# Thresholded attention with a hardswish MLP: an order in periods of two slots for the work between the score matmuls

## The chip, the cores and the metric

The kernel runs on one core of a Trainium2 chip. The metric is the device time of one launch. Before the change three runs took 568.69, 568.73 and 570.11 us; the median is 568.73 us. The profiled execution took 568.41 us, of which 566.6 us lie between its first and its last instruction, at a mean granted TensorE clock of 0.994.

## What is computed

Eight batches of eight heads, 576 rows, head size 64, then an MLP on the joined heads (512 to 2048 to 512):

```python
scores = q @ k.T / 8                              # per head, 576 x 576
thresh = max(scores, -1) - tau                    # tau = 0.02
scores = where(scores >= thresh, scores, -1e9)
attn = exp(scores - max(scores, -1)); attn /= sum(attn, -1) + 1e-9
x = (attn @ v), heads joined                      # 4608 x 512
h = x @ w_in                                      # 4608 x 2048
out = (h * clip(h + 3, 0, 6) / 6) @ w_out         # 4608 x 512
```

## The kernel before

The 64 heads form 32 pairs and 16 quads (a quad is four heads, two pairs of one batch). A quad has nine slots. Slots 0 to 3 are the four blocks of 128 rows of its first pair, slots 4 to 7 those of its second, and slot 8 holds the last 64 rows of all four heads. A slot is one tile of 128 rows by 2 x 576 columns: head `a=0` and head `a=1`. There are 144 slots, numbered n.

The order is written out by hand; no scheduler moves anything. Each engine works through its own queue in the order in which the loop `for n, sl in enumerate(queue)` issues instructions, and semaphores tie the queues. One turn of the loop handles several slots at once:

- ScalarE: the exponentials of slot n-1 (`sm_exp`, L311), a rectifier of the MLP if it falls to ScalarE (`mm1_relu`, L386), then the threshold of slot n (`sm_mask`, L306).
- VectorE: the row maxima of slot n+1 (`sm_max`, L299; they also copy the scores out of PSUM), the copies left in `waiting`, a rectifier if it falls to VectorE (L388), the gate (`mm1_gate`, L401), the reciprocal of slot n-1's row sums (`sm_recip`, L314), then the transposes of q and k for later quads (L238, L244, one VectorE instruction each), and the copies out of PSUM of the attention product (`av_main` L354, `av_rest` L364) and of the output (`osb`, L420).
- GpSimd: the bias of the threshold (L302) and the normalisation of slot n-1 (`sm_norm`, L319), whose result a transposing DMA on SyncE's queue brings into `pT` or `pR` for the attention product (L327).
- TensorE: one `mm1` item (L378, eight matmuls of 256 columns, or L373, four of 512), in even slots two parts of `mm2` (L412, eight matmuls of 512), the products `av_main` (slots 3 and 8, L343 and L346) and `av_rest` (slot 4), and the scores (L284).

From slot N1 = 22 on the scores are issued in odd slots only, those of slot n+3 first and then those of n+2: `for m in (n + 3, n + 2): scores(m)`. The copies in `waiting` run in odd slots only (at the end of an odd slot, or after the maxima of the next slot when they arose in an even one). Two sets of PSUM columns hold scores. Even slots use one set, odd slots another, and `scores(m)` can start when `sm_max(m-2)` has read its set:

```python
def score_col(n, a):
    return (704 if first(n) else 128) + (0 if a else 1536)
```

The last 256 columns of an odd slot's scores lie in banks 2 and 5. These two banks also serve, in turns (`bank()`), the products of `av` and the transposes by TensorE. `mm1` has one bank, HB = 6, so the next `mm1` waits for the gate of the last; `mm2` has bank 7.

The loads of q and k are prepared by `load_quad` and started one after another at the end of a slot (`start(loads, 1)`, SyncE's queue). For quads 0 to 3 TensorE transposes q and k (`by_pe`), for later quads VectorE does, 128 x 576 at a time; the last 64 rows of k (`transpose_rest`, L254) always go through TensorE, and ScalarE copies them out (L219, two copies).

Which slots have the rectifier on ScalarE, and when the transposes come, is written as sets of slots:

```python
r = mm1_relu(h, on_act=(slot in ((0, 2, 4, 8) if quad < 2 * NB else (0, 1, 3, 4) if quad % 2 else (0, 4, 5, 8))))
t0 = 3 if quad % 2 and quad > 1 else 4
t1 = -1 if quad % 2 == 0 and quad > 2 else 0 if quad else 1
```

`t0` is the slot of a quad in which q of the next quad's first pair is transposed, followed by its k and the rest; `t1` and `t1 + 1` are the slots of q and k of a quad's own second pair, with q one slot ahead at some quad borders. Since a quad has nine slots, these slots have both parities. After the loop a tail finishes the MLP of the last batches.

Of the kernel before, what the change touches and what calls it, by code (L numbers as in the profile page):

```python
# [20 lines left out]
def kernel(  # L21
# [17 lines left out]
    NQUAD = B * H // 4  # L39
    NSLOT = 9  # L40
    NB = 2
    N1 = 22
# [28 lines left out]
    qkT = {}  # L71
# [124 lines left out]
    def alloc_qk(quad):  # L196
        qkT[quad] = (qk_pool.tile([P, 2, S], F32, tag="qT", name="qT"),
                     qk_pool.tile([P, 2, S + 64], F32, tag="kT", name="kT"))

    def qT_of(pair):  # L200
        return qkT[pair // 2][0][:, pair % 2, :]

    def kT_of(pair):
        return qkT[pair // 2][1][:, pair % 2, :]
# [17 lines left out]
    def by_pe(pair):  # L222
        return pair // NPAIR < NB
# [8 lines left out]
    def transpose_q(pair):  # L232
        nq = nat[pair // 2][0]
        if by_pe(pair):
            pb = main_pe(nq[:, 0:1024].rearrange("p (t h d) -> p t h d", h=4, t=4), pair)
            return lambda: nc.vector.tensor_copy(out=qT_of(pair)[:, 0:512], in_=pb)
        n = pair % 2
        nc.vector.transpose(out=qT_of(pair), in_=nq[:, n * S:(n + 1) * S])  # L238

    def transpose_k(pair):  # L240
        if not by_pe(pair):
            n = pair % 2
            km = nat[pair // 2][1][:].rearrange("p t h d -> p (t h d)")
            nc.vector.transpose(out=kT_of(pair)[:, 64:576], in_=km[:, n * 512:(n + 1) * 512])  # L244
            return None
        pb = main_pe(nat[pair // 2][1], pair)
        return lambda: copy_out(kT_of(pair)[:, 64:576], pb)
# [43 lines left out]
    def sm_max(sl):  # L291
        sl.s = s_pool.tile([P, 2, S], F32, tag="s", name="s")
        sl.m = stat_pool.tile([P, 2], F32, tag="m", name="m")
        sl.bias = stat_pool.tile([P, 2], F32, tag="bias", name="bias")
        sl.rsum = stat_pool.tile([P, 2], F32, tag="rsum", name="rsum")
        sl.rinv = stat_pool.tile([P, 2], F32, tag="rinv", name="rinv")
        for i in range(2):
            c0 = score_col(sl.n, i)
            nc.vector.tensor_scalar(out=sl.s[:, i, :], in0=ps_flat[:, c0:c0 + S],  # L299
                                    scalar1=1.0, scalar2=None, op0=Alu.mult, op1=Alu.max,  # L300
                                    accum_out=sl.m[:, i:i + 1])
        nc.gpsimd.tensor_scalar(out=sl.bias[:], in0=sl.m[:], scalar1=-scale, scalar2=tau, op0=Alu.mult, op1=Alu.add)  # L302
# [10 lines left out]
    def sm_recip(sl):  # L313
        nc.vector.reciprocal(out=sl.rinv[:], in_=sl.rsum[:])  # L314
# [15 lines left out]
    def pe_transpose(sl):  # L330
        pb = ps_flat[:, HB * 512:HB * 512 + S].bitcast(BF16).rearrange("p (c t) -> p c t", t=P)
        pn = sl.pn[:].rearrange("p a b -> p (a b)")
        for c in range(9):
            nc.tensor.transpose(pb[:, c, :], pn[:, c * P:(c + 1) * P], identb[:])
        return lambda: nc.vector.tensor_copy(out=sl.dst, in_=pb)
# [47 lines left out]
    def mm1_relu(hps, on_act):  # L383
        r = r_pool.tile([P, 512], F32, tag="r", name="r")[:]
        if on_act:
            nc.scalar.activation(out=r, in_=hps, func=Act.Relu, bias=three[:])  # L386
        else:
            nc.vector.tensor_scalar(out=r, in0=hps, scalar1=3.0, scalar2=0.0, op0=Alu.add, op1=Alu.max)  # L388
        return r

    def mm1_gate(item, hps, r):
        b, ni, c0 = item
        if c0 is None:
            if ni % 8 == 0:
                odd[0] = go_pool.tile([P, 1024], BF16, name="go")
            out = odd[0][:, ni % 8 * P:ni % 8 * P + 512]
        else:
            c0 += (b % 2) * (S + 64)
            out = gbuf[:, ni:ni + 2, c0:c0 + 256]
            r, hps = (x.rearrange("p (n w) -> p n w", n=2) for x in (r, hps))  # L400
        nc.vector.scalar_tensor_tensor(out=out, in0=r, scalar=6.0, in1=hps, op0=Alu.min, op1=Alu.mult)  # L401
        if c0 is None and ni % 8 == 4:
            nc.sync.dma_start_transpose(out=gbuf[:, ni - 4:ni + 4, 512:512 + P], in_=odd[0][:])
# [45 lines left out]
    evict = transpose_k(0)  # L449
# [25 lines left out]
    sm_max(queue[0])  # L475
    scores(1)

    prev = None
    part = 0
    waiting = []  # L480
    for n, sl in enumerate(queue):
        quad, slot = sl.quad, sl.slot
        b, g = divmod(quad, 2)
        now = n
        if slot in (0, 4):
            pts[2 * quad + slot // 4] = pt_pool.tile([P, 9, 512], BF16, tag="pT", name="pT")
        if slot == 8:
            ptr[quad] = ptr_pool.tile([P, 9, P], BF16, tag="pR", name="pR")
        for ahead in {0: (1, 2), 9: (3,), 16: (4,)}.get(n, (quad + 2,) if quad > 2 and slot == 4 else ()):
            if ahead < NQUAD:  # L490
                load_quad(ahead)
        if slot == 0 and g == 1 and b + 1 < B:
            load_v(b + 1)
        if prev is not None:
            for i in range(2):
                sm_exp(prev, i)
        if n + 1 < len(queue):
            sm_max(queue[n + 1])
        for copy in waiting:
            copy()  # L500
        waiting = []

        if todo1:
            item, then = todo1.pop(0)
            h = mm1(item)
            r = mm1_relu(h, on_act=(slot in ((0, 2, 4, 8) if quad < 2 * NB else (0, 1, 3, 4) if quad % 2 else (0, 4, 5, 8))))
            mm1_gate(item, h, r)
            todo2.extend(then)
        copies = pe_transpose(queue[n - 2]) if n > 1 and queue[n - 2].on_chip else None
        if prev is not None:  # L510
            sm_recip(prev)
        if copies:
            copies()
        for _ in range(2 if n % 2 == 0 and todo2 else 0):
            bb, mt, part = todo2.pop(0)
            mm2_part(bb, mt, part)
        for i in range(2):
            sm_mask(sl, i)
        evict = []
        nxt = 2 * quad + 2  # L520
        t0 = 3 if quad % 2 and quad > 1 else 4
        t1 = -1 if quad % 2 == 0 and quad > 2 else 0 if quad else 1
        if slot == t1 or slot == 8 and quad % 2 and 1 < quad < NQUAD - 1:
            evict.append(transpose_q(2 * (quad + slot // 8) + 1))
        if slot == t1 + 1:
            evict.append(transpose_k(2 * quad + 1))
        if n == 3:
            evict.append(transpose_rest(0, of_k=False))
        if slot == 3 and quad > 0:
            waiting.append(av_main(2 * quad - 1))  # L530
        elif slot == 4 and quad > 0:
            waiting.append(av_rest(quad - 1))
            if quad % 2 == 0:
                todo1.extend(moe_of(quad // 2 - 1))
        if t0 <= slot < t0 + 3 and quad + 1 < NQUAD:
            if slot == t0:
                alloc_qk(quad + 1)
                evict.append(transpose_q(nxt))
            elif slot == t0 + 1:
                evict.append(transpose_k(nxt))  # L540
            else:
                evict.append(transpose_rest(quad + 1))
        if slot == 8:
            waiting.append(av_main(2 * quad))
        for out_of_psum in evict:
            if out_of_psum:
                out_of_psum()
        if part == 3:
            waiting.append(lambda tile=(bb, mt): late.extend(mm2_out(*tile, on_act=False)))
            part = 0  # L550
        if n < N1 or n % 2:
            for copy in waiting:
                copy()
            waiting = []
        if n == 0:
            warm_up(8)
        if n <= N1:
            scores(n + 2)
        elif n % 2:
            for m in (n + 3, n + 2):  # L560
                if m < len(queue):
                    scores(m)
        if n < 8:
            warm_up(6)
        if prev is not None:
            sm_norm(prev)
        flush()
        if n == 0:
            start(loads, 2)
        elif n not in (4, 12, 15, 18, 21) and not 23 < n < 34:  # L570
            start(loads, 1)
        if n < 4 or 15 < n < 20 or n > 33:
            start(vcasts, 1)
        else:
            start(casts, 2 if n in (5, 8, 11, 14) or 21 < n < 28 else 1)
        prev = sl
# [80 lines left out]
```

## Time and profile before

| what | value |
|---|---|
| median of three runs | 568.73 us |
| TensorE busy | 532.5 us |
| ScalarE busy | 450.4 us |
| VectorE busy | 444.0 us |
| GpSimd busy | 277.2 us |
| row maxima, L299 | 288 x 749 ns |
| threshold, L306; exponential, L311 | 288 x 763 ns; 288 x 670 ns |
| gate, L401 | 128 x 687 ns to `g`, 16 x 687 ns to `go` |
| rectifier on VectorE, L388; on ScalarE, L386 | 67 x 685 ns; 77 x 685 ns |
| reciprocal, L314 | 144 x 158 ns |
| transposes on VectorE, q L238; k L244 | 24 x 757 ns; 24 x 692 ns |
| normalisation, L319 | 288 x 745 ns |
| VectorE's maxima idle for scores (L284) | 40.4 us |
| ScalarE's rectifier idle for mm1 (L378) | 48.5 us |
| VectorE's gate idle for ScalarE's rectifier | 24.0 us |

Durations of neighbours on one engine overlap a little, so the pace, from start to start, is shorter than the duration: the two maxima of a slot start 0.68 us apart at 0.75 us each. Idle time of an engine costs something only if its next instruction lies on the path that sets the end. A matmul counts as busy while it waits in the array behind another one, so TensorE's share of busy time is not its share of peak.

### The profile page before, as it was taken

To read this page: it belongs to the slowest core of one execution; us is meant where nothing else is said; L and a number is where in the kernel's file an instruction comes from. 1 tells how busy PE (TensorE), PEld (TensorE's weight loads), DVE (VectorE), ACT (ScalarE), POOL (GpSimd) and SP (SyncE) were. 2 spreads that over 40 slices of the span, in tenths; PEclk is the share of its full clock that TensorE was granted. 3 is DMA by queue.
4 is the path that set the end of the run, shared out by engine and by line. 5 is a ranking of instruction groups with operands and counts; after the bars stand their busy time and mean duration, and the time that the engine had idled before them with its cause. 6 is when DMAs were issued, how large, how long until landed. Compare 5 with 4: busy or idle time off the path is not lost.

```text
span 566.6 us, 11592 instructions
## 1 busy us (share of the span) xinstructions
PE 532.5 (94%) x3865; PEld 321.2 (57%) x3865; DVE 444.0 (78%) x1099; ACT 450.4 (79%) x977; POOL 277.2 (49%) x502
## 2 busy tenths in 40 slices
PE   8999988999968999999999999999999999999997
PEld 6765555655535556556555556556555556664663
DVE  3788878888876988888888988888888898882541
ACT  3999969888988788878898888977897888991540
POOL 1788868556463445644455454644355444460000
PEclk9999999999988999999999999999999999999999
DMA  5999989779999768987899878987789875553212
GB/s 120 135 162 152 169 136 186 121 124 160 177 158 171 142 117 145 184 142 137 148 148 184 154 133 139 188 148 142 129 142 193 155 133 111 104 104 97 60 35 74
DMA packets 316587, 78.73 MB, mean 139 GB/s; under 512 B 299504, under 2 KB 312048, under 8 KB 316528
## 3 DMA queue, kind: packets, MB, share of 16 engines
q1 hardware_dynamic: 297920, 68.69, 68.6%
q0 software_dynamic: 17408, 8.92, 14.4%
q8 instruction: 30, 0.49, 0.4%
q10 hardware_dynamic: 1200, 0.39, 0.3%
q14 instruction: 29, 0.24, 0.1%
HBM read 36.70 MB, written 9.44 MB: 81 GB/s over the span
## 4 chain that ended last, share of the span: by engine, by line
PE 45%; DVE 23%; issue 7%; ACT 6%; DMA 4%; POOL 2%; SPq 2%; POOLq 0%; DVEq 0%
PE ps L284 17%; PE ps L378 12%; DVE s L299 10%; PE ps L412 9%; PE ps L343 3%; ACT r L386 3%; DVE r L388 3%; DVE g L401 3%; POOL pn L319 2%; DMA pT<-pn 2%; ACT s L306 2%; DVE qT L238 2%; ACT s L311 1%; DVE kT L244 1%; DVE rinv L314 1%
## 5 line engine op out<-in xcount | busy, mean ns | idle before, releaser
L319 POOL TENSOR_SCALAR pn<-s,rinv 128x576 bf16<-128x576 f32 x288 | 210.9, 745 | 153.9 <-DVE rinv L314 63.7
L299 DVE TENSOR_SCALAR_CACHE_REDUCE s<-ps 128x576 f32<-128x576 f32 x288 | 205.3, 749 | 47.7 <-PE ps L284 40.4
L306 ACT ACTIVATE s<-s,bias 128x576 f32<-128x576 f32 x288 | 205.9, 763 | 6.3 <-POOL bias L302 6.0
L284 PE MATMUL ps<-kT,qT 64*128 64x192 f32 (+7 forms) x1280 | 193.9, 422 | 8.5 <-DVE s L299 4.7
L311 ACT ACTIVATE s<-s 128x576 f32<-128x576 f32 x288 | 192.5, 670 | 0.3
L284 PEld LDWEIGHTS ps<-kT,qT 64*128 64x128 f32 (+1 forms) x1280 | 116.4, 176 | 75.1 <-DVE s L299 23.1
L378 PE MATMUL ps<-xT,w_in_sb 128*128 128x256 bf16 x1024 | 131.3, 274 | 6.7 <-DVE g L401 5.1
L412 PE MATMUL ps<-w_out_sb,g 128*128 128x512 bf16 x576 | 133.5, 379 | 0.0
L378 PEld LDWEIGHTS <-w_in_sb 128*128 128x128 bf16 x1024 | 94.6, 98 | 51.5 <-issue 36.5
L401 DVE SCALAR_TENSOR_TENSOR g<-r,ps 128x512 bf16<-128x512 f32 x128 | 87.9, 687 | 26.1 <-ACT r L386 24.0
L386 ACT ACTIVATE r<-ps,three 128x512 f32<-128x512 f32 x77 | 52.7, 685 | 59.1 <-PE ps L378 48.5
L412 PEld LDWEIGHTS <-g 128*128 128x128 bf16 x576 | 56.2, 98 | 57.8 <-issue 0.7
L302 POOL TENSOR_SCALAR bias<-m 128x2 f32<-128x2 f32 x144 | 27.1, 188 | 78.0 <-DVE s L299 59.0
L311 ACT ACTIVATION_READ_ACCUMULATOR s<-s 128x1 f32 x288 | 54.5, 189 | 0.0
L388 DVE TENSOR_SCALAR r<-ps 128x512 f32<-128x512 f32 x67 | 45.9, 685 | 0.6 <-PE ps L378 0.6
L420 DVE TENSOR_SCALAR osb<-ps 128x512 f32<-128x512 f32 x31 | 21.2, 684 | 24.4 <-PE ps L412 24.4
L343 PE MATMUL ps<-pT,vm 128*64 128x512 bf16 x256 | 34.6, 393 | 3.6 <-DMA pT<-pn 3.6
L343 PEld LDWEIGHTS <-vm 128*64 128x64 bf16 x512 | 18.1, 112 | 25.7 <-issue 16.0
L354 DVE CAST xT<-ps 128x512 bf16<-128x512 f32 x32 | 21.7, 679 | 4.5 <-PE ps L346 3.7
L299 DVE DVE_READ_ACCUMULATOR s<-ps 128x1 f32 x288 | 23.8, 83 | 0.0
L219 ACT COPY kT<-ps 64x128 f32<-64x128 f32 (+1 forms) x29 | 8.5, 293 | 18.3 <-PE ps L254 11.0
L314 DVE RECIPROCAL rinv<-rsum 128x2 f32<-128x2 f32 x144 | 22.7, 158 | 0.0
(56 smaller groups left out, 242.0 us busy)
## 6 DMA issues: line engine op xcount, KB each, us to landing
out_dram<-osb SPq DMA_DIRECT2D x31, 256.0 KB, 2.5
nq<-in_q_dram SPq DMA_DIRECT2D x96, 72.0 KB, 3.0
km<-in_k_dram SPq DMA_DIRECT2D x96, 64.0 KB, 2.8
vm<-in_v_dram POOLq DMA_DIRECT2D x16, 256.0 KB, 5.3
km<-in_k_dram SPq DMA_DIRECT2D x16, 128.0 KB, 4.3
w_in_sb<-in_moe_w_in_dram POOLq DMA_DIRECT2D x16, 128.0 KB, 4.5
w_out_sb<-in_moe_w_out_dram POOLq DMA_DIRECT2D x16, 128.0 KB, 4.3
pT<-pn SPq DMA_TRANSPOSE x117, 3.5
```

What stands on the lines that cost most here:

```text
L284: nc.tensor.matmul(ps_flat[rows, c0:c0 + w], qT_of(pair)[a * 64:(a + 1) * 64, q0:q0 + rows.stop - rows.start], kT_of(pair)[a * 64:(a + 1) ...
L299: nc.vector.tensor_scalar(out=sl.s[:, i, :], in0=ps_flat[:, c0:c0 + S], scalar1=1.0, scalar2=None, op0=Alu.mult, op1=Alu.max, accum_out=sl ...
L306: nc.scalar.activation(out=s, in_=s, func=Act.Prelu, bias=sl.bias[:, i:i + 1], scale=scale, alpha=REJECT)
L311: nc.scalar.activation(out=s, in_=s, func=Act.Exp, accum_out=sl.rsum[:, i:i + 1])
L314: nc.vector.reciprocal(out=sl.rinv[:], in_=sl.rsum[:])
L319: nc.gpsimd.tensor_scalar(out=pn[:, i, :], in0=sl.s[:, i, :], scalar1=sl.rinv[:, i:i + 1], scalar2=1.0, op0=Alu.mult, op1=Alu.mult)
L343: nc.tensor.matmul(pb[a * 64:(a + 1) * 64, :], vm[:, 2 * hp + a, c * D:(c + 1) * D], pT[:, 5 * a + c, cols], start=(c == 0), stop=False)
L378: nc.tensor.matmul(ps[:, hb, n * 256:(n + 1) * 256], w_in_sb[:, ki, (ni + n) * P:(ni + n + 1) * P], xT[b][:, ki, c0:c0 + 256], start=(ki = ...
L386: nc.scalar.activation(out=r, in_=hps, func=Act.Relu, bias=three[:])
L388: nc.vector.tensor_scalar(out=r, in0=hps, scalar1=3.0, scalar2=0.0, op0=Alu.add, op1=Alu.max)
L401: nc.vector.scalar_tensor_tensor(out=out, in0=r, scalar=6.0, in1=hps, op0=Alu.min, op1=Alu.mult)
L412: nc.tensor.matmul(o_ps[0], gbuf[:, ni, mt * P:(mt + 1) * P], w_out_sb[:, ni, :], start=(ni == 0), stop=(ni == NI - 1))
```

## The change

The order is given a period of two slots from slot 22 on. Even slots hold only the maxima, the rectifier and the gate on VectorE. Odd slots hold all transposes of q and k, the copies, the reciprocals of two slots and, on GpSimd, the norms of two slots; their rectifier is made by ScalarE, and their gate comes after the transposes. So that all transposes fall on odd slots, a table `turns` gives the slot of each: for quad 3 and later, every second slot from `first_odd` on, in the order q, k, rest, q, k. This starts up to four slots earlier than before, so `load_quad` of quad 6 and later is called at slot 0 in place of slot 4. The aim is to take out of even slots what the next odd slot's maxima would wait for.

```diff
+    turns = {1: [("q", 1)], 2: [("k", 1)], 3: [("rest", 0)]}
...
+    for quad in range(1, NQUAD):
+        n0 = quad * NSLOT
+        first_odd = n0 - 9 + quad % 2
+        for i, (job, of) in enumerate((("q", 2 * quad), ("k", 2 * quad), ("rest", quad),
+                                       ("q", 2 * quad + 1), ("k", 2 * quad + 1))):
+            turn_at(n0 + (-5, -4, -3, 0, 1)[i] if quad < 3 else first_odd + 2 * i, job, of)
+
     prev = None
+    ready = []
...
-        for ahead in {0: (1, 2), 9: (3,), 16: (4,)}.get(n, (quad + 2,) if quad > 2 and slot == 4 else ()):
+        for ahead in {0: (1, 2), 9: (3,), 16: (4,)}.get(n, (quad + 2,) if quad > 2 and slot == (4 if quad == 3 else 0) else ()):
...
             sm_max(queue[n + 1])
+        even = n >= N1 and n % 2 == 0
+        for old in ready:
+            sm_recip(old)
         for copy in waiting:
             copy()
         waiting = []
 
+        gate = None
         if todo1:
             item, then = todo1.pop(0)
             h = mm1(item)
-            r = mm1_relu(h, on_act=(slot in ((0, 2, 4, 8) if quad < 2 * NB else (0, 1, 3, 4) if quad % 2 else (0, 4, 5, 8))))
-            mm1_gate(item, h, r)
+            r = mm1_relu(h, on_act=not even)
+            gate = lambda: mm1_gate(item, h, r)
             todo2.extend(then)
+        if gate and even:
+            gate()
         copies = pe_transpose(queue[n - 2]) if n > 1 and queue[n - 2].on_chip else None
-        if prev is not None:
+        if prev is not None and n < N1:
             sm_recip(prev)
...
-        nxt = 2 * quad + 2
-        t0 = 3 if quad % 2 and quad > 1 else 4
-        t1 = -1 if quad % 2 == 0 and quad > 2 else 0 if quad else 1
-        if slot == t1 or slot == 8 and quad % 2 and 1 < quad < NQUAD - 1:
-            evict.append(transpose_q(2 * (quad + slot // 8) + 1))
-        if slot == t1 + 1:
-            evict.append(transpose_k(2 * quad + 1))
-        if n == 3:
-            evict.append(transpose_rest(0, of_k=False))
+        for job, of in turns.get(n, ()):
+            if job == "k":
+                evict.append(transpose_k(of))
+            elif job == "q":
+                if of // 2 not in qkT:
+                    alloc_qk(of // 2)
+                evict.append(transpose_q(of))
+            else:
+                evict.append(transpose_rest(of, of_k=of > 0))
+        if n >= N1 and not even:
+            sm_recip(prev)
+            if gate:
+                gate()
...
-        if t0 <= slot < t0 + 3 and quad + 1 < NQUAD:
-            if slot == t0:
-                alloc_qk(quad + 1)
-                evict.append(transpose_q(nxt))
-            elif slot == t0 + 1:
-                evict.append(transpose_k(nxt))
-            else:
-                evict.append(transpose_rest(quad + 1))
...
         if prev is not None:
-            sm_norm(prev)
+            ready.append(prev)
+        if not even:
+            for old in ready:
+                sm_norm(old)
+            ready = []
```

## The prediction

> **What bounds the kernel now.** I read the busy times first, then the windows, then one pair of slots in order of time, then the waits.
>
> ```profile
> PE 532.5 (94%) x3865; PEld 321.2 (57%) x3865; DVE 444.0 (78%) x1099; ACT 450.4 (79%) x977; POOL 277.2 (49%) x502
> ...
> PE 45%; DVE 23%; issue 7%; ACT 6%; DMA 4%; POOL 2%; SPq 2%; POOLq 0%; DVEq 0%
> ```
>
> TensorE looks full and also leads the chain of waits, but half of that chain lies elsewhere. Its 94% hides slack: the 16 score matmuls of a pair of slots took 2.14 us from the first start to the next group's start where nothing held them, and up to 2.81 us where their second half started late, all of it "busy". So I took the pair apart. The steady part runs from slot 22 (70.7 us) to slot 143 (501.7 us); after it a tail of 65 us is almost pure TensorE and the change leaves it alone. The pattern repeats every 36 slots: slots 90 to 126 take 129.1 us, so 7.17 us a pair. One pair on VectorE:
>
> ```profile
> 341.22 0.69 DVE L401 SCALAR_TENSOR_TENSOR g<-r,ps 128x512 bf16<-128x512 f32 x1
> 341.82 0.16 DVE L314 RECIPROCAL rinv<-rsum 128x2 f32<-128x2 f32 x1
> 341.90 0.74 DVE L299 TENSOR_SCALAR_CACHE_REDUCE s<-ps 128x576 f32<-128x576 f32 x1
> 342.56 0.08 DVE L299 DVE_READ_ACCUMULATOR s<-ps 128x1 f32 x1
> 342.56 0.75 DVE L299 TENSOR_SCALAR_CACHE_REDUCE s<-ps 128x576 f32<-128x576 f32 x1
> 343.24 0.08 DVE L299 DVE_READ_ACCUMULATOR s<-ps 128x1 f32 x1
> 343.24 0.69 DVE L388 TENSOR_SCALAR r<-ps 128x512 f32<-128x512 f32 x1
> 343.96 0.69 DVE L401 SCALAR_TENSOR_TENSOR g<-r,ps 128x512 bf16<-128x512 f32 x1
> 344.56 0.16 DVE L314 RECIPROCAL rinv<-rsum 128x2 f32<-128x2 f32 x1
> 345.36 0.76 DVE L299 TENSOR_SCALAR_CACHE_REDUCE s<-ps 128x576 f32<-128x576 f32 x1 [0.64 <-PE ps L284]
> ...
> 347.38 0.69 DVE L401 SCALAR_TENSOR_TENSOR g<-r,ps 128x512 bf16<-128x512 f32 x1 [0.58 <-ACT r L386]
> 347.99 0.16 DVE L314 RECIPROCAL rinv<-rsum 128x2 f32<-128x2 f32 x1
> 348.06 0.74 DVE L299 TENSOR_SCALAR_CACHE_REDUCE s<-ps 128x576 f32<-128x576 f32 x1
> ```
>
> The odd slot starts at 341.90 with the maxima of an even slot. They free the banks of the next even scores, and TensorE issues all four score halves at the end of the odd slot. VectorE then waits (0.64 us) for the first of them, and the even slot's own VectorE work starts at 345.36. In the even half VectorE has nothing to wait for but its own queue. So a pair is a loop: **odd half** (341.90 to 345.36, 3.46 us: maxima, then scores on TensorE, with the rest of the odd slot's VectorE work beside them) plus **even half** (345.36 to 348.06, 2.70 us: everything in VectorE's queue counts). Reading the starts of the maxima over slots 90 to 126, the 18 even halves sum to 52.4 us (mean 2.91) and the odd halves to 76.7 us (mean 4.26).
>
> SyncE's queue matters once, after slot 34:
>
> ```profile
> 122.53 2.99 SPq L99 DMA_DIRECT2D km<-in_k_dram  x4
> 125.62 2.95 SPq L327 DMA_TRANSPOSE pT<-pn  x1
> 128.62 2.20 SPq L94 DMA_DIRECT2D nq<-in_q_dram  x4
> ```
>
> These are the first loads of quad 5. VectorE begins slot 37 at 126.92, so the queue runs behind the program here.
>
> **What the Trainium skill says.** "Perfetto Trace Analysis", Identifying the Most-Contended Engine, says matmul busy share is a poor measure of headroom because pipelined work looks different in a trace; the 2.14 against 2.81 us above agrees. "DMA: Bandwidth & Descriptors", Issuing engines are not separate DMA queues, calls the sequencer's time to start a DMA usually small beside the DMA; this trace differs: a transpose holds SyncE 1.3 us, four q loads 2.2 us, and over slots 90 to 126 its DMA instructions fill 87% of the time. "TensorE: Matmul & The Clock Gate", What's actually happening, says an idle array falls to half clock; after the 2.7 us wait for pT at 164.9 us eight mm1 matmuls take 1.89 us instead of 1.05, which agrees.
>
> **The even half.** It keeps two maxima, rectifier and gate. In the trace these pace at 0.68, 0.68, 0.72 and 0.60 us: 2.69 us. Out go one reciprocal (0.07 of pace), transposes (0.62 to 0.67) and, where ScalarE made the rectifier, the wait for it (0.6 above), though 0.72 of VectorE rectifier comes in there. 2.91 - 2.69 = 0.22 us, times 61 pairs: **-13.4 us**. The rectifier must find mm1 done: mm1 starts 0.2 us after the half begins, is readable 0.87 + 0.2 later, and the rectifier is due at 1.36, so it just fits.
>
> **The odd half.** It now holds two maxima 1.36, two reciprocals 0.14, a gate 0.6 whose rectifier is ScalarE's, nearly always one transpose 0.66, and as before the copies of av (0.62), av_rest (0.22) and osb (0.6, every other pair). The plain sum, 2.75 us, or 3.35 with osb, lies beside TensorE's path. That path: mm1 starts 0.12 after the half begins (the gate before it has to end; the 0.07 of reciprocal or 0.67 of transpose that lay between them is gone), scores 0.95 later, first half readable 2.44 after that (342.92 to 345.36): 3.53 us. Cases in 18 slots, before and after:
> - three plain ones (even quad slots 1, 7; odd quad slot 2): 3.39 to 3.46, now 3.53.
> - av in the odd slot (even quad slot 3, odd quad slot 8): av's ten matmuls take 1.2 on TensorE, so scores start at 2.2 and end at 4.64. The av copy lies in bank 2 or 5, which the last quarter of the odd scores also uses; it ends at 3.4, or 4.0 with osb, against 3.8 when that quarter starts. Bank 2 costs up to 0.3 then, bank 5 nothing. Before 4.57 and 5.25, now 4.79 and 4.64.
> - av in the even slot before (odd quad slot 0): TensorE is late by 1.2. Two transposes and an av copy still fit (4.06 against 4.6). Before 4.74, now 4.6.
> - slot-8 scores of odd quads (slot 6): 4.05, now 4.1.
> - k-rest transposes, moved from even to odd slots (even quad slot 5, odd quad slot 4). ScalarE does rectifier, two masks and only then the two copies (0.53), ready 3.75 after the half begins, or 4.9 in the odd quad where mm1 itself is 1.2 late. The last quarter would start at 3.5 and 4.6. So +0.25 to +0.3 each: before 4.33 and 5.2, now 4.35 and 5.44.
>
> The sum is 38.5 against 38.4: **+0.7 us** over the run.
>
> ScalarE gets eight rectifiers more (VectorE: from 67 to 59 in the order of instructions). "ScalarE: Activation LUTs", What ACT_TABLE_LOAD costs, prices one at about 0.28 + 0.00083 x 512 = 0.71 us; the trace has 0.685. Per pair it needs four exps and four masks at 1.33 a pair and one rectifier at 0.58: 5.9 us, under 6.2, the shortest pair, so no net cost.
>
> **Norms** go in twos at the end of odd slots. Reciprocal at 1.44, four norms at 0.745: POOL is done 4.7 us into the pair, and the next bias is due at about 5.1. Score buffer reuse needs the first two by 3.5; they end at 3.25. The pT transposes get up to a slot later; av reads them three slots on or more. Cost nothing, but with only 0.25 us to spare.
>
> **Earlier loads and transposes.** Only quad 5 is tight: its q transpose moves from slot 40 to 37, due near 127.6, while its load stands behind the transposes of slots 33 and 34. With norms in pairs the load would issue at 124.3 to 126.5 and land 3.0 later (the median in the list of issues), 129.5; with the queue as before, about 133. Stall 2 to 5.5 us, I take 2.5: **+2.5 us**. Against it SyncE catches up, so that the 2.7 us wait at 164.9 may shrink; counted as nothing. Slots before 22 keep their order.
>
> Sum: 568.7 - 13.4 + 0.7 + 2.5 = 558.5, say **559 us**.
>
> **Rivals.**
> - *Odd half too full, 576 us.* Gate, rectifier and copies of the odd slot are now all late in it, and mm1 of the even slot waits for that gate in its one bank. If each odd half grows by 0.3 us, that is 61 x 0.3 = 18: 568.7 - 13.4 + 18 + 2.5. For it: the trace's 24.0 us of gates waiting for ScalarE and the narrow margins above. Against: the transpose now stands between reciprocal and gate and covers the rectifier.
> - *Both halves gain, 551 us.* If osb, av copies and k-rest copies all hide, heavy odd halves fall to TensorE's 4.3 or so: about 1 us less in 18 slots, 7 in all, and the wait at 164.9 us vanishes (-3): 549 to 552.
> - *No change, 568 us.* SyncE at 87% becomes the bound: pairs can't drop below 0.87 x 7.17 = 6.2, and contiguous loads in slots 0 to 4 lag; the 13 us return as waits for pT.
>
> **Chances.** Forecast 0.50, both halves 0.20, odd half too full 0.22, no change 0.08. Faster than 567.0 are the first two and small parts of the others (0.04): 0.74. Within 0.3% is most of the last: 0.06. Slower is most of the third: 0.20. Range 550 to 575: it leaves out part of the second case below and part of the third above, about 2 in 10.
>
> **What would show it.** Right: even halves of 2.69 with no wait for ScalarE; maxima waiting for scores about as before; the k-rest copies releasing scores late; one VectorE wait for nq of 2 to 5 us near 128. Wrong: gates of odd slots waiting for the rectifier, mm1 of even slots waiting for a gate, maxima waiting for norms, av waiting for pT.

## The result and the profile after

The changed kernel took 569.89 us, the median of four runs (569.01 to 570.68), beside 569.03 for the kernel before (568.69 to 570.11). The ratio is 1.0012, with a 95% interval of 0.9989 to 1.0034: no change, where 559 us was forecast. Yet a good part of what was forecast did happen. Here is the page of the changed kernel, busy times and then the chain of waits by engine:

```profile
PE 528.5 (93%) x3823; PEld 324.9 (57%) x3865; DVE 436.3 (77%) x1092; ACT 454.9 (80%) x984; POOL 277.0 (49%) x502
...
PE 49%; DVE 21%; issue 5%; DMA 3%; ACT 3%; POOL 2%; SPq 2%; DVEq 0%; POOLq 0%
```

The chain has less VectorE (23 to 21) and ScalarE (6 to 3) and more TensorE (45 to 49): the order did move what it was meant to move. The same place in a quad as in the prediction, read on VectorE's timeline (start, duration, and in brackets the idle time before and what ended it):

```profile
347.70 0.75 DVE L299 TENSOR_SCALAR_CACHE_REDUCE s<-ps 128x576 f32<-128x576 f32 x1
...
348.38 0.75 DVE L299 TENSOR_SCALAR_CACHE_REDUCE s<-ps 128x576 f32<-128x576 f32 x1
...
349.06 0.16 DVE L314 RECIPROCAL rinv<-rsum 128x2 f32<-128x2 f32 x1
349.14 0.76 DVE L238 STREAM_TRANSPOSE qT<-nq 128x576 f32<-128x576 f32 x1
349.82 0.12 DVE L314 RECIPROCAL rinv<-rsum 128x2 f32<-128x2 f32 x1
349.86 0.66 DVE L401 SCALAR_TENSOR_TENSOR g<-r,ps 128x512 bf16<-128x512 f32 x1
351.20 0.76 DVE L299 TENSOR_SCALAR_CACHE_REDUCE s<-ps 128x576 f32<-128x576 f32 x1 [0.68 <-PE ps L284]
...
352.56 0.69 DVE L388 TENSOR_SCALAR r<-ps 128x512 f32<-128x512 f32 x1
353.28 0.69 DVE L401 SCALAR_TENSOR_TENSOR g<-r,ps 128x512 bf16<-128x512 f32 x1
353.89 0.75 DVE L299 TENSOR_SCALAR_CACHE_REDUCE s<-ps 128x576 f32<-128x576 f32 x1
```

The even half runs from 351.20 to 353.89: 2.69 us, two maxima, rectifier and gate with nothing between, and the rectifier waits for nobody. The odd half, 347.70 to 351.20, takes 3.50, and in it both reciprocals, the transpose and the gate fit beside TensorE's scores, with 0.68 us to spare. In this pair the design does what it was made for: 6.19 us, where the same two slots took 6.16 before, since that pair had been a light one; the gain lies in the heavier even halves, which in slots 90 to 126 were up to 3.38 before and are 2.69 to 3.02 now.

So I took the whole steady part apart in the prediction's own unit, the differences between the starts of the maxima, from those of slot 22 to those of slot 143. A half has the number of the turn of the loop that issues its maxima, which are those of the next slot: half 37 begins with the maxima of slot 38. "Start of slot 22" is the start of slot 22's own maxima, so the first half counted is number 21; there are 61 odd halves and 60 even ones.

| sum, us | before | changed | difference |
|---|---|---|---|
| start of slot 22 | 70.7 | 71.6 | +1.0 |
| even halves | 173.0 | 161.8 | -11.2 |
| odd halves | 258.1 | 271.3 | +13.2 |
| slot 143 to the end of the span | 64.9 | 64.2 | -0.7 |

It is also clear where: from the maxima of slot 54 to those of slot 126 it took 253.9 us instead of 257.8, a gain, while from slot 22 to slot 54 it took 120.8 instead of 114.3, a loss. The +13.2 of the odd halves is made of these:

| where | us |
|---|---|
| slot 37, 3.39 to 8.11 | +4.7 |
| slot 4 of odd quads (31, 49, 67, 85, 103, 121) | +4.2 |
| slots 21 to 29, around the transposes of quad 3 | +2.7 |
| slot 53 | +1.1 |
| slot 5 of even quads (41, 59, 77, 95, 113) | +1.0 |
| slot 39, right after slot 37's wait | +0.8 |
| all others | -1.3 |

**Slot 37.** VectorE's timeline, then SyncE's, then TensorE's, all of the changed kernel:

```profile
135.78 0.78 DVE L238 STREAM_TRANSPOSE qT<-nq 128x576 f32<-128x576 f32 x1 [4.68 <-DMA nq<-in_q_dram]
```

```profile
121.75 2.66 SPq L99 DMA_DIRECT2D km<-in_k_dram  x4
124.99 6.31 SPq L327 DMA_TRANSPOSE pT<-pn  x2
131.35 2.20 SPq L94 DMA_DIRECT2D nq<-in_q_dram  x4
```

```profile
137.24 1.87 PE L378 MATMUL ps<-xT,w_in_sb 128*128 128x256 bf16 x8 [4.55 <-DVE g L401]
```

The q transpose of quad 5 was due at 131.1. Its load stood behind two pT transposes that held SyncE from 124.99 to 131.30 (3.6 and 2.6 us, where 1.3 is usual), and was issued at 131.35. The DMA engines were crowded there: between 120 and 132 us pT took 5.0 us from issue to landing, by the median, against 3.5 over the run. VectorE waits 4.68 us, behind it the gate, behind the gate mm1: TensorE idles for 4.55. Its next eight mm1 matmuls then take 1.87 us instead of 1.05, at half the clock, as shown below, and that is how slots 38 and 39 become longer too.

**Slot 4 of an odd quad**, here slot 103, on TensorE, ScalarE and VectorE:

```profile
368.77 1.05 PE L378 MATMUL ps<-xT,w_in_sb 128*128 128x256 bf16 x8
369.66 0.27 PE L254 MATMUL ps<-identf,kr 128*128 128x128 f32 x1
...
372.34 0.70 PE L284 MATMUL ps<-kT,qT 64*128 64x256 f32 x4 [0.27 <-ACT kT L219]
```

```profile
369.86 0.69 ACT L386 ACTIVATE r<-ps,three 128x512 f32<-128x512 f32 x1 [1.40 <-PE ps L378]
370.44 1.43 ACT L306 ACTIVATE s<-s,bias 128x576 f32<-128x576 f32 x2
371.77 0.52 ACT L219 COPY kT<-ps 64x128 f32<-64x128 f32 x2
```

```profile
373.17 0.76 DVE L299 TENSOR_SCALAR_CACHE_REDUCE s<-ps 128x576 f32<-128x576 f32 x1 [1.71 <-PE ps L284]
```

TensorE transposes the rest of k at 369.66 into the bank that the turn gives. ScalarE copies it out only after a rectifier, which waits for mm1 (1.40 us idle), and two masks. The last quarter of the odd slot's scores needs the same bank, so it starts at 372.34, when the copies end. In TensorE's queue everything else stands behind these four matmuls. The half takes 5.81 us where it took 4.97. Not all of the 0.84 is the copies': with them out of the way (in the experiment "Rest of k in even slots") the same half takes 5.16. There the scores start 2.83 us into the half, and before the change 2.15: av of slot 102 stands in front of them, and the even half before it is shorter by a transpose that used to run beside it.

**Slots 27 to 29.** Quad 3 is transposed by TensorE, its second pair too, into the same banks. The new table has its q and k in slots 19, 21, 25 and 27 in place of 22, 23, 27 and 28 (nowhere does it bring a transpose forward by more than three slots, not four as said above), so that all of them stand in odd slots, in front of the scores. ScalarE, then TensorE:

```profile
94.99 0.57 ACT L219 COPY kT<-ps 128x512 f32<-128x512 f32 x1
```

```profile
95.61 0.70 PE L284 MATMUL ps<-kT,qT 64*128 64x256 f32 x4 [0.43 <-ACT kT L219]
96.25 1.05 PE L378 MATMUL ps<-xT,w_in_sb 128*128 128x256 bf16 x8
99.26 1.78 PE L378 MATMUL ps<-xT,w_in_sb 128*128 128x256 bf16 x8 [1.97 <-DVE g L401]
```

It is the same wait for ScalarE's copy in bank 2 or 5, followed here by an idle stretch of 1.97 us and by matmuls at a lower clock.

**The clock.** The trace has the clock that was granted to TensorE, as a share of full speed. It is the third number from the end in these lines (stretch in us, length, busy time of the engines, clock, DMA share, GB/s):

```profile
99.39:102.80 3.41, 3.41 (x16) 2.09 (x16) 2.59 (x8) 1.90 (x5) 2.04 (x4) 0.50 0.94 168
136.93:140.34 3.41, 3.10 (x12) 1.77 (x12) 2.78 (x7) 1.23 (x2) 2.07 (x4) 0.50 0.55 82
174.48:181.31 6.83, 6.14 (x43) 3.46 (x45) 2.59 (x9) 2.46 (x6) 3.12 (x5) 0.50 0.88 161
```

These three stretches, in slots 29, 38 and 49, are the only ones at half clock between 20 and 500 us: 13.7 us in all, where the kernel before has one of 6.8 (slot 49). Matmuls take at most about twice as long in them (eight of av 1.92 us for 1.05), so by themselves they cost no more than 6.8 and 3.4 us.

### The profile page after: what moved, and what is told of

Its sections match the earlier page's. It is cut to its first block, busy times and chain, and to the rows that moved or that the text cites. A ratio compares the mean times of both kernels' runs of the same rounds, so it can differ in the third digit from the quotient of the medians.

```text
span 568.9 us, 11517 instructions
## 1 busy us (share of the span) xinstructions
PE 528.5 (93%) x3823; PEld 324.9 (57%) x3865; DVE 436.3 (77%) x1092; ACT 454.9 (80%) x984; POOL 277.0 (49%) x502
## 4 chain that ended last, share of the span: by engine, by line
PE 49%; DVE 21%; issue 5%; DMA 3%; ACT 3%; POOL 2%; SPq 2%; DVEq 0%; POOLq 0%
PE ps L284 17%; PE ps L378 14%; PE ps L412 12%; DVE s L299 10%; PE ps L343 4%; DVE r L388 4%; DVE g L401 4%; POOL pn L319 2%; ACT s L306 2%; DMA pT<-pn 2%; PE ps L373 1%; DVE qT L238 1%; DVE osb L420 1%; DMA nq<-in_q_dram 1%; PE ps L346 1%
## 5 line engine op out<-in xcount | busy, mean ns | idle before, releaser
L284 PE MATMUL ps<-kT,qT 64*128 64x384 f32 (+7 forms) x1280 | 190.5, 423 | 5.4 <-DVE s L299 2.1
L284 PEld LDWEIGHTS ps<-kT,qT 64*128 64x128 f32 (+1 forms) x1280 | 118.1, 177 | 65.2 <-issue 14.1
L378 PE MATMUL ps<-xT,w_in_sb 128*128 128x256 bf16 x1024 | 132.9, 276 | 15.8 <-DVE g L401 15.7
L412 PE MATMUL ps<-w_out_sb,g 128*128 128x512 bf16 x540 | 128.0, 381 | 2.0 <-issue 0.3
L386 ACT ACTIVATE r<-ps,three 128x512 f32<-128x512 f32 x85 | 58.2, 687 | 69.8 <-PE ps L378 52.1
L388 DVE TENSOR_SCALAR r<-ps 128x512 f32<-128x512 f32 x59 | 40.5, 686 | 1.4 <-PE ps L378 0.6
L314 DVE RECIPROCAL rinv<-rsum 128x2 f32<-128x2 f32 x144 | 21.0, 148 | 1.9 <-ACT s L311 1.9
L238 DVE STREAM_TRANSPOSE qT<-nq 128x576 f32<-128x576 f32 x24 | 18.2, 758 | 4.7 <-DMA nq<-in_q_dram 4.7
```

Of the source, the lines that this page charges most:

```text
L284: nc.tensor.matmul(ps_flat[rows, c0:c0 + w], qT_of(pair)[a * 64:(a + 1) * 64, q0:q0 + rows.stop - rows.start], kT_of(pair)[a * 64:(a + 1) ...
L378: nc.tensor.matmul(ps[:, hb, n * 256:(n + 1) * 256], w_in_sb[:, ki, (ni + n) * P:(ni + n + 1) * P], xT[b][:, ki, c0:c0 + 256], start=(ki = ...
L412: nc.tensor.matmul(o_ps[0], gbuf[:, ni, mt * P:(mt + 1) * P], w_out_sb[:, ni, :], start=(ni == 0), stop=(ni == NI - 1))
```

## The experiments

**Theory A**: the new order gains about 11 us in the even halves, and three separate local faults give it back: the late first load of quad 5, the bank of the k-rest copies, quad 3's early transposes. **Theory B**: SyncE's queue is the real bound, so whatever is mended comes back as waits for pT. Every ratio is against the kernel before on the same chip, with its 95% interval.

### Load quad 5 earlier

The load of quad 5 is prepared at slot 30, and loads may start from then on; all else as changed.

```diff
-        for ahead in {0: (1, 2), 9: (3,), 16: (4,)}.get(n, (quad + 2,) if quad > 2 and slot == (4 if quad == 3 else 0) else ()):
+        for ahead in {0: (1, 2), 9: (3,), 16: (4,), 30: (5,)}.get(n, (quad + 2,) if quad > 3 and slot == 0 else ()):
...
-        elif n not in (4, 12, 15, 18, 21) and not 23 < n < 34:
+        elif n not in (4, 12, 15, 18, 21) and not 23 < n < 30:
```

> Edit to the changed kernel: the loads of quad 5 are prepared at slot 30 and started from slot 30 on (before: 31 and 34). Theory A (the gain of the even halves is real, and single waits outside the steady part ate it): VectorE's 4.7 us wait for nq in slot 37 goes, and the odd half of slot 37 falls from 8.11 to 3.4 us; the time falls by 4 to 5 us to about 565. Theory B (SyncE's queue limits slots 22 to 54 whatever the order): the wait goes but comes back as waits of the attention product for pT by slot 54, and the time stays within 1.5 us of the changed kernel's 569.9.

Measured: 563.76 us, ratio 0.9904 (0.9884 to 0.9925). Slot 37 went from 8.11 to 3.43, the slot after it from 3.37 to 2.69, and slot 39 from 4.50 to 3.78. The wait for nq is gone and nothing took its place there. Slot 49 fell from 9.14 to 4.92 as well, which was not expected; the time fell by 6.1 us by the ratios, where 4 to 5 were. Slot 45 rose from 4.66 to 5.97 and slot 53 from 6.07 to 6.86. In slot 53 av waits 2.15 us for pT; in slot 45's half it starts at 157.18, just after a transpose issued at 153.56 has landed (3.5 us later). So waits for pT moved, as theory B said, but only a small part of the gain went back.

### Rest of k in even slots

The rest of k is transposed one slot later, in an even slot.

```diff
-            turn_at(n0 + (-5, -4, -3, 0, 1)[i] if quad < 3 else first_odd + 2 * i, job, of)
+            turn_at(n0 + (-5, -4, -3, 0, 1)[i] if quad < 3 else first_odd + 2 * i + (job == "rest"), job, of)
```

> Edit to the changed kernel: for quads 3 and later the transposes of the last rows of k stand one slot later, in even slots, so that ScalarE's two copies no longer stand between the rectifier of an odd slot and the scores of the same slot. Theory A: the odd halves of odd quads' slot 4 fall from 5.8 to about 5.0 us and those of even quads' slot 5 by up to 0.3, even halves stay at 2.69; over six odd quads and seven even ones 5 to 6 us less, about 564. Rival: the copies then delay the masks and exps of the even slot, the next rectifier on ScalarE comes 0.5 later, and nothing is gained (569 to 570).

Measured: 567.43 us, ratio 0.9982 (0.9969 to 0.9994). Slot 103 went from 5.81 to 5.16 and its like with it (67: 5.78 to 5.12; 85: 5.82 to 5.17), and slot 113 from 4.90 to 4.79. The even halves after slot 5 of an even quad fell from 2.90 and 3.02 to 2.69, so that nearly all are 2.69 now. The odd halves gained only 2.4 us in all, and the time fell by 1.7 us by the ratios where 5 to 6 were expected, since slot 39 (4.50 to 5.24) and slot 51 (4.00 to 5.70) took some back, though none of their own jobs is moved. Slot 51's scores run at half clock here (184.78 to 188.20 us).

### Quad 3 as before

The transposes of quad 3 keep their old slots.

```diff
-            turn_at(n0 + (-5, -4, -3, 0, 1)[i] if quad < 3 else first_odd + 2 * i, job, of)
+            turn_at(n0 + (-5, -4, -3, 0, 1)[i] if quad < 4 else first_odd + 2 * i, job, of)
```

> Edit to the changed kernel: quad 3, whose q and k TensorE transposes, keeps its transposes at the old slots (22, 23, 24, 27, 28). Theory A: TensorE's transposes and ScalarE's copy in front of the odd scores in slots 19 to 27 cost about 1 us before slot 22 and 2 to 3 us in slots 22 to 31 (with slower matmuls after TensorE's idle time in slot 28); the time falls by 2 to 4 us to about 567. Rival: these slots are late for another cause, the missing mm2 work that lets TensorE idle and cool in even slots; then slot 29 still takes 5 us and the time falls by less than 1 us.

Measured: 568.83 us, ratio 0.9997 (0.9981 to 1.0012): no gain in time. The slots themselves did improve: slot 21 from 4.17 to 3.73, 27 from 4.57 to 3.94, 29 from 5.07 to 3.43. The maxima of slot 54 begin at 187.9 us against 192.4; of these 4.5 us, 2.4 were there at those of slot 33, and the rest comes from slot 49 (9.14 to 5.84), less 1.0 that slot 39 lost. Then the half that begins there, slot 53's, took 10.90 us instead of 6.07. TensorE's timeline of this kernel:

```profile
192.38 1.92 PE L343 MATMUL ps<-pT,vm 128*64 128x512 bf16 x8 [3.35 <-DMA pT<-pn]
...
194.66 3.97 PE L284 MATMUL ps<-kT,qT 64*128 64x384 f32 x16
```

av waits 3.35 us for pT, and the 16 score matmuls after it take 3.97 us instead of about 2.1 to 2.8, at half clock (191.43 to 198.25 us). SyncE had km loads before the transposes of pT there. So an engine that comes earlier to a late transfer only waits longer: theory B holds, at this place.

### All three

> The three edits before in one: early loads of quad 5, k-rest transposes in even slots, quad 3 at its old slots. Theory A: the gains add up, 4.5 + 5.5 + 3 = 13 us less than the changed kernel, about 557 us, with even halves still at 2.69: this is the version in which the even halves' 11 us show. Theory B (SyncE or TensorE takes over): less than half the sum, 563 us or more.

The three edits above in one kernel. Measured: 556.96 us, ratio 0.9777 (0.9748 to 0.9806). By the ratios the three alone are worth 6.1, 1.7 and 0.9 us against the changed kernel, 8.7 in sum; together they give 13.4. They are not independent: what one saves, a late transfer or a stretch at half clock can take back, as slot 53 of quad 3's edit and slot 51 of the k-rest edit have just shown. Even halves sum to 160.4 and odd ones to 259.7. What stands out still is slot 45 (5.51), slot 51 (5.59) and slot 53 (8.08). In slot 53 TensorE shows what it was:

```profile
182.54 1.55 PE L343 MATMUL ps<-pT,vm 128*64 128x512 bf16 x8 [1.73 <-DMA pT<-pn]
```

### The rectifiers alone

To the kernel before, with nothing moved: the rectifier of odd slots on ScalarE, of even slots on VectorE.

```diff
-            r = mm1_relu(h, on_act=(slot in ((0, 2, 4, 8) if quad < 2 * NB else (0, 1, 3, 4) if quad % 2 else (0, 4, 5, 8))))
+            r = mm1_relu(h, on_act=n % 2 == 1)
```

> Edit to the kernel before, one part of the change alone: the rectifier is VectorE's in even slots and ScalarE's in odd slots; transposes, reciprocals and norms stay where they were. Theory A (an even half counts everything in VectorE's queue): even halves without a transpose take 2.76, those 8 of 18 with one 3.4, a sum of 55 us over slots 90 to 126 against 52.4 before; the heavy odd halves of slot 8 in odd quads fall by 0.3 to 0.6; in all 571 to 574 us, slower than before. Rival: VectorE's load counts, 8 rectifiers of 0.72 less, so 563 us.

Measured: 572.48 us, ratio 1.0070 (1.0044 to 1.0095). The even halves with a transpose are 3.38 to 3.44 and those without 2.76: the sums forecast from the paces of single instructions, 2.69 + 0.07 for the reciprocal and 0.62 to 0.67 for a transpose. The old table had put rectifiers on ScalarE in nearly all even slots that held a transpose of q or k. So bringing rectifiers in without taking transposes out costs time; taking transposes out alone was not run.

### Norms and reciprocals in every slot

All three edits, but reciprocals and norms slot by slot, as before the change.

```diff
-        for old in ready:
-            sm_recip(old)
...
-        if prev is not None and n < N1:
+        if prev is not None and (n < N1 or even):
             sm_recip(prev)
...
-            ready.append(prev)
-        if not even:
-            for old in ready:
-                sm_norm(old)
-            ready = []
+            sm_norm(prev)
```

> Edit to the version with the three corrections: reciprocal and norms of slot n-1 in every slot n, as before the change, in place of two at a time in odd slots. Theory A: the even halves get a reciprocal back, 2.69 to 2.76, 61 times 0.07 = 4.3 us, about 561 us; odd halves stay. Rival: the pairing delays the norms of odd slots by a slot and so the pT transposes, and its waits (maxima for norms 9.9 us, products for pT 4.1 us) outweigh the reciprocal: without it 554 us or less.

Measured: 559.01 us, ratio 0.9835 (0.9799 to 0.9871). The even halves are 2.76 instead of 2.69, all but a few, 4.4 us in sum (160.4 to 164.8), and 0.07 is the pace of one reciprocal. So in the even halves that small instruction is worth what the prediction took. But the odd halves take most of it back: between the maxima of slots 90 and 126 each of them is 0.01 to 0.08 us shorter here than with all three edits, 75.3 against 76.1 in sum, while the even ones are longer, 49.7 against 48.4. The period of two slots for reciprocals and norms is worth 0.5 us there, not the 1.3 of the even halves. Slot 53 took 10.48 in the profiled execution, so the difference in time is rougher than that in halves.

### Loads in every second slot

All three edits, and from slot 36 on loads start only in even-numbered slots of a quad, so that at most every second slot puts loads before the transposes.

```diff
-        elif n not in (4, 12, 15, 18, 21) and not 23 < n < 30:
+        elif n not in (4, 12, 15, 18, 21) and not 23 < n < 30 and (n < 36 or slot % 2 == 0):
```

> Edit to the version with the three corrections: from slot 36 on loads of q and k are started in slots 0, 2, 4, 6 and 8 of a quad in place of slots 0 to 4. Theory A (what is left over steady pace in slots 45 to 53 is products waiting for pT behind a run of loads in SyncE's queue): the odd halves of slots 45, 51 and 53 (5.5, 5.6 and 8.1 us) fall towards 4.7, 4.1 and 4.6, the time to about 552. Rival: SyncE has as much to do as before and is behind anyway, the waits only move; 556 to 558.

Measured: **553.25 us** (551.88 to 554.01), ratio 0.9740 (0.9711 to 0.9770), the fastest of all, though its interval just touches that of all three edits (0.9748 to 0.9806). Slot 45 went from 5.51 to 4.75, 51 from 5.59 to 4.06, 53 from 8.08 to 4.64; slot 47 rose from 3.43 to 5.11. Not all of this is transfers. In slot 51 with all three edits 24 score matmuls (slot 53 has twice as many as other slots) took 4.33 us, where they take 2.8 here; in slot 47 here 16 took 4.21, after an idle stretch of 1.75. That is the clock: it is 0.50 from 172.72 to 176.13 us there and from 158.61 to 162.02 here. From the end of a slot's norms to the issue of its transpose, SyncE is up to 11.6 us late in the changed kernel (slot 47), 9.4 with all three edits (slot 48), and 5.5 here (slot 45); in the kernel before it was 8.8 (slot 44). Its chain of waits, by engine:

```profile
PE 55%; DVE 22%; issue 5%; POOL 5%; DMA 1%; ACT 1%; SPq 1%; DVEq 0%; POOLq 0%
```

DMA has fallen from 3% to 1%, and among the waits of this kernel there is none of av for pT; the changed kernel's list has two lines of them:

```profile
PE ps L343 <- DMA pT<-pn: 4.1, 2, 2.7
...
PEld L343 <- DMA pT<-pn: 3.8, 3, 3.0
```

Theory B was right that the order in SyncE's queue costs time in slots 36 to 54, and wrong that this can't be mended: the queue is about as full here, for between the maxima of slots 90 and 126 its DMA instructions fill 87% of the time, and 86% in the kernel before.

### The other bank

The early load, and the turn of the two banks starts with the other one.

```diff
-    turn = 0
+    turn = 1
```

> Edit to the changed kernel with the early loads of quad 5: the two banks of the attention product and of the transposes change places (turn starts at 1). In the changed kernel the rest of k of odd quads (slot 4) stands in the bank that the last quarter of head a=0's scores needs, and it costs 0.85 us a time; that of even quads (slot 5) stands in a=1's bank and costs 0.03 in slot 95. Theory (the price of ScalarE's late copy depends on which head's bank it holds, since VectorE reads a=0 first and a=1 0.68 us later): slot 103 falls from 5.81 to about 5.45, slot 95 rises from 3.98 to about 4.3, the time changes by under 1 us. Rival (TensorE's queue stops for either head alike): slot 103 stays at 5.8 and slot 95 at 4.0.

Measured: 561.51 us, ratio 0.9862 (0.9822 to 0.9902). It changes nothing in what is done, only which of banks 2 and 5 holds it. Slot 103 fell from 5.81 to 5.27, all even halves but a few are 2.69, while slot 95 rose from 3.98 to 4.66 and slot 113 from 4.90 to 5.72. Against the early load alone (0.9904) the time fell by 2.4 us by the ratios, whose intervals overlap; the halves of the two profiled executions sum to the same, 426.7 us, so the change of under 1 us that was expected is not refuted. TensorE and ScalarE in slot 103 of this kernel:

```profile
363.70 2.75 PE L284 MATMUL ps<-kT,qT 64*128 64x384 f32 x16
```

```profile
365.18 0.52 ACT L219 COPY kT<-ps 64x128 f32<-64x128 f32 x2
```

The same copies, as late after mm1 as before, no longer split the scores: 16 matmuls run in one stretch, because the bank with the late copies is needed by head a=1, whose quarter comes last. In even quads it is now head a=0 that meets it, and these slots pay.

### The loads alone

The kernel before, with the loads of the fastest version and nothing else.

```diff
+        for ahead in {0: (1, 2), 9: (3,), 16: (4,), 30: (5,)}.get(n, (quad + 2,) if quad > 3 and slot == 0 else ()):
...
+        elif n not in (4, 12, 15, 18, 21) and not 23 < n < 30 and (n < 36 or slot % 2 == 0):
             start(loads, 1)
```

> Edit to the kernel before: the loads of the best version (quad 5 from slot 30, from slot 36 on in even slots of a quad), all else as before. It tells how much of the best version's 15 us is the order in periods of two slots and how much the loads. Theory A: only the wait of slot 49 (8.4 us against 5.0 in later odd quads) goes, 3 to 4 us, about 565 us, so that the order itself is worth about 12 us once nothing else waits. Rival: the loads alone give most of it, 558 us or less.

Measured: 564.66 us, ratio 0.9916 (0.9883 to 0.9948). Nearly all of it is slot 49, 8.36 to 4.35, whose av waited 2.7 us for pT before and which then ran at half clock; this kernel has no stretch at half clock between 20 and 500 us. So SyncE's queue already mattered in the kernel before at a second place, where the prediction saw one, after slot 34. The loads are worth about 4.8 us to the old order, and the rest of the fastest version, 10.0 by the ratios and 11.4 by the medians (taken on two chips), is the order's own, with its k-rest and quad 3 mended. By halves it is plainer still: from this kernel to the fastest, even halves 172.1 to 160.4 (-11.7), odd halves 254.7 to 255.3 (+0.6).

## Why the prediction was wrong

The forecast was 10.2 us less; the profiled span became 2.3 us longer (566.6 to 568.9). Of these 12.5 us, 10.0 are in the odd halves, which with the stall were to lose 3.2 and lost 13.2, 2.2 in the even halves, and 1.0 ahead of slot 22, less 0.7 in the tail. So the steps that failed are those about the odd slots: the cost of the k-rest transposes, quad 3's transposes, which had no term, and the size of the stall in slot 37.

- **The even half: right in mechanism and nearly in size.** Forecast 2.69 us; it is 2.69 in all but a few. The sum came to -11.2 and not -13.4, since I took the mean of slots 90 to 126 (2.91) for 61 halves, and there are 60, with a mean of 2.88; and since after slot 5 of an even quad mm1 comes late from the k-rest copies (2.90 and 3.02), which the edit of the rest in even slots removed.
- **"k-rest transposes, moved from even to odd slots ... So +0.25 to +0.3 each ... now 4.35 and 5.44": a term mis-sized.** Slot 4 of odd quads became 5.81. The copies were as late as forecast (4.9 us into the half), but there they cost 0.65 and not 0.3, for 5.16 was reached without them. Two readings were wrong. VectorE doesn't wait for the first score half that is issued: the loop issues the scores of slot n+3 first, and the maxima that come next are those of slot n+2, head a=0 first, so a late last quarter of that head holds VectorE. And "Bank 2 costs up to 0.3 then, bank 5 nothing" has the banks the wrong way round: by `score_col` the last 256 columns of head a=0 are in bank 5, those of a=1 in bank 2. With the banks changed over, slot 4 of odd quads (now bank 2) gave 5.27 and slot 5 of even quads 0.7 to 0.8 more than before; the late av copies followed too: slot 107, in bank 5, took 4.83 and then 4.63, slot 111 4.64 and then 4.83. The halves with k-rest grew by 5.2 us in both kinds of quads, where the prediction's own before and after come to 1.5; of slot 49's share, 0.8, part is its wait for pT.
- **"Slots before 22 keep their order": failed.** Quad 3 is transposed by TensorE and copied by ScalarE and VectorE, and the table moved it to slots 19 to 27. That cost 0.6 us in slot 19 (2.69 to 3.29; the other 0.4 by which slot 22 starts later is within the spread of kernels that keep these slots, 69.9 to 71.2 us) and 2.7 in slots 21 to 29, part of it at half clock; the prediction had no term for it. The edit that undid it gave 2.4 us up to slot 33, and the time was lost again in slot 53, to pT and the clock.
- **"Stall 2 to 5.5 us, I take 2.5": a term mis-sized.** The stall was at the place and on the tile named, but 4.68 us; and it left TensorE at half clock, after which slots 38 and 39 took 1.4 more (0.68 and 0.72, against the early load's), within the 1.7 us that 3.41 us at half clock can cost. The value taken rested on SyncE issuing the load as soon as norms came in pairs; instead two transposes of 6.31 us together stood ahead of it, and it was issued at 131.35, where 124.3 to 126.5 was forecast.
- **"The 2.7 us wait at 164.9 may shrink; counted as nothing": right for that wait, but a term was missing.** It stayed (2.70 us, now ending at 175.17), and a second one of 1.4 us came in slot 53, which grew by 1.1; "pT transposes get up to a slot later ... Cost nothing" did not hold there. Here the rival "No change" was partly right: SyncE did cost time, but only in slots 36 to 54. After slot 53 it held nothing back that mattered: from there to the maxima of slot 126 all three edits took 244.4 us, and with the spaced loads 244.3.
- **The other rivals.** "Odd half too full" did not happen for its reason. These are waits of the changed kernel (total, number, longest):

```profile
DVE g L401 <- ACT r L386: 11.0, 30, 1.8
DVE s L299 <- POOL pn L319: 9.2, 13, 1.2
...
PEld ps L284 <- ACT kT L219: 7.8, 13, 0.9
```

Gates waited for ScalarE's rectifier 24.0 us before and 11.0 now, so the transpose between mostly covers it, as that rival's "against" said. Maxima waiting for norms (POOL still reading the score buffer) rose from 3.9 to 9.2: the margin of 0.25 us was too thin in places, yet six of the halves that end in such a wait (33, 51, 69, 87, 105, 123) took 4.00, no more than the 4.05 before. The third line is for the most part the k copies' bank. "Both halves gain" gave 551; with the loads and transposes mended the same order takes 553.25.
- **The odd half's +0.7 us** was not met in the changed kernel, because of the terms above; the cases without k-rest did come within 0.2 us of the forecast between the maxima of slots 90 and 126 (plain ones 3.43 to 3.50 for 3.53, slot 6 of odd quads 4.00 for 4.1). With everything mended it is met in number, +0.6 between the loads alone and the fastest version, but by luck: slot 47, which then ran at half clock, has 1.7 of it, and between the maxima of slots 90 and 126 the odd halves fell, from 77.0 to 76.1.

Open: how much of slots 39 to 54 is the clock and how much the transfer. Half the time at half clock bounds the first, 3.4 us in the changed kernel's slot 49, but they often come together.

## What to carry to other kernels

Cost a reordering in the unit that limits it (here the half between two starts of maxima), and then walk once through its edges: the first slots in which it applies, the buffers that are filled by another engine, and the queue that feeds it. A table that is moved as a whole takes along entries that follow another path, such as quad 3's. When a correct gain doesn't show, mend the late transfer first: until then each engine that gets faster only waits longer, and single repairs look worth less (8.7 us) than they are together (13.4).

## What the runs showed of the hardware

- A wait can cost more than its length on TensorE. After 4.55 us of idling eight mm1 matmuls took 1.87 us instead of 1.05, after 3.35 us eight av matmuls 1.92 instead of 1.05. "TensorE: Matmul & The Clock Gate", HAM oscillation — how this bites in real kernels, puts the limit at gaps of about 3.4 us; here shorter ones sufficed, 2.70 us (half clock from 174.48) and 1.97 (from 99.39), while at 181.31 of the kernel with quad 3 as before the same 1.97 did not (1.03 us).
- It is not the gap alone that decides. The same page, What's actually happening, says that activity is counted in a window of about 3.41 us that runs freely. The traces agree: between 20 and 500 us the stretches at half clock of every kernel are 3.41 or 6.83 us long, and in each kernel they start whole multiples of 3.41 us apart (99.39, 136.93 and 174.48 in the changed kernel, 11 each time). Laid out on that grid between 20 and 500 us, the eleven kernels have eleven windows at full clock in which the profile shows TensorE busy under 43% of the time, and half clock followed every one (42% before 99.39). It followed none in which TensorE was busy over 59%. Between these both happened (46% before 181.19 in the kernel with quad 3 as before, without a drop; 49% before 158.61 in the fastest), and the runs don't show what decides there.
- Two copies, equally late, made an odd quad's slot 4 take 5.81 us or 5.27, by which of two PSUM banks they came from; without them it took 5.16. The one is needed in the middle of what VectorE waits for, the other behind it.
- SyncE's time to start transfers is a resource like an engine: one pT transpose holds it 1.3 us, four q loads 2.2, and between 100 and 175 us of the fastest version its DMA instructions fill 91% of the time without a wait for pT in the list.
